# Second layer of an attention-plus-two-layers kernel: five nearly equal token groups, staging lent slot by slot, an operand store moved to GpSimd, weight sums a step ahead

## The chip, the core and the metric

The kernel runs on one NeuronCore of a Trainium2 chip. Five engines run side by side, each through its own queue in order: TensorE (PE in the profile; its weight loads are PEld), VectorE (DVE), ScalarE (ACT), GpSimd (POOL) and SyncE (SP), which here issues transfers only. A transfer (DMA) is issued by one of the queues and moved by 16 DMA engines. The metric is the device time of one execution in microseconds.

## The reference

Attention with a softmax over the feature axis of q and over the sequence axis of k, then two feed-forward layers on 4608 tokens of 512 features:

```python
kv = einsum('bhsd,bhse->bhde', softmax_seq(k), v)    # 8 x 8 heads, 576 x 64
x = einsum('bhsd,bhde->bhse', softmax_feat(q), kv)   # then heads side by side: 4608 x 512
x = square(relu(x @ w_in)) @ w_out       # first layer,  512 -> 2048 -> 512
h = x @ w_in2                            # second layer, 512 -> 2048
out = (h * sigmoid(h)) @ w_out2          #               2048 -> 512
```

All is float32. Each product on TensorE is made of three: both operands are split into a high part (rounded to the engine's float32r format) and the rest (low), and high x high, high x low and low x high are summed.

## The kernel before

The first layer runs in nine blocks of 512 tokens (`NB = 9`, `layer_in`, `layer_out`). It is not touched, except for what lies beside its last block.

The second layer multiplies 2 x 2 block matrices with seven products instead of eight (the Strassen-Winograd scheme): each operand has four quarters, and sums of quarters make up seven left operands (`PRODUCTS`: A11, S3, S2, S1, A12, A22, S4) and seven right ones (B11, T3, T2, T1, B21, N4, B22). Phase 2 is the product with `w_in2`, phase 3 the one with `w_out2`. Tokens are handled in groups `u`; the width of a group is the number of columns that stream through TensorE in one matmul. `supers` makes pairs of first-layer blocks, so that there are four groups of 512 columns and one of 256 (the ninth block alone). Each group has 56 steps in phase 2 and 56 in phase 3 (seven products x `NG = 8` feature groups `j`), and each step is six matmuls. So there are 2 x 56 x 6 = 672 matmuls for each group, 3360 in all: 2688 of 512 columns and 672 of 256. `LAST_LONG` puts the 256-column group fourth in phase 2 and a 512-column one last; in phase 3 the 256-column group is last.

Phase 2 goes by pairs of feature groups (`k` = 0, 1) and 14 steps for each pair (`PAIR`). `hidden_after` takes the results out of PSUM: products 0 and 2 are copied to four rooms that are kept for it (`keep`), product 1 to slot A22 of a tile `st` of seven slots; Silu follows, then the sums S1 to S4. A tile is stored to `g2d` by GpSimd in three transfers (2, 3 and 2 slots). `stpool` has two such tiles, one for each `k`: the next pair takes its tile at product 1 (`st[k] = stpool.tile(...)`), which waits until the stores of the pair before have landed. A function appended to `soon` runs one step later.

SBUF rooms of 512 columns (`NU = 89`) are lent and taken back in order. `a_load` fetches a left operand (SP), `a_split` makes its high part on ScalarE (tile `ah`) and its low part on VectorE (`al`, in place). Weights: `quarters` loads four quarters of a rounded weight from `wd` (SP), `weight_sums` makes T1, T2, T3 and N4 on GpSimd in one temporary (`wt`), and `weight_split` makes high and low parts (ScalarE, VectorE). `seven` does all that for one `j` of phase 2 beside the last block of the first layer. For phase 3 `raw_weights` loads and makes the first sums, and `product_weights` goes product by product through all `j` and makes the later sums between the splits. These are generators: each step of the loop advances those in `doing`, and starts others from `todo` while there is room. From the last block on (`pinned`) every engine's queue is in the order of the program.

Of the kernel before, what the change touches and what calls it, by code (L numbers as in the profile page):

```python
# [25 lines left out]
def kernel(  # L26
# [56 lines left out]
    P = 128  # L83
# [47 lines left out]
    def back(*ts):  # L131
# [7 lines left out]

    supers = [tuple(range(i, min(i + 2, NB))) for i in range(0, NB, 2)]  # L140
    NS = len(supers)
    x2d = [
        [dpool.tile([P, 7, len(bl) * HB], F32, name=f"x2d{u}_{e}") for e in range(2)]
        for u, bl in enumerate(supers)
    ]
    g2d = [
        [dpool.tile([P, 7, len(bl) * HB], F32, name=f"g2d{u}_{j}") for j in range(NG)]
        for u, bl in enumerate(supers)
    ]
# [114 lines left out]

    def weight_sums(w, t, which):

        b11, b21, b22 = (f32(w[n])[:, hi_] for n in (0, 4, 6))
        b12, s = t[:, lo_], t[:, hi_]
        if which == 0:
            gp.tensor_tensor(s, b12, b11, op=ALU.subtract)  # L270
            gp.tensor_tensor(b12, b22, b12, op=ALU.subtract)
        elif which == 1:
            gp.tensor_tensor(s, b22, s, op=ALU.subtract)
        else:
            gp.tensor_tensor(s, b21, s, op=ALU.subtract)

    def weight_split(ph, x, n, w, t):

        if n in w:
            src = f32(w[n])[:, hi_]  # L280
        else:
            w[n] = room(F32R, f"w{PRODUCTS[n][1]}")
            src = t[:, lo_ if n == 1 else hi_]
        ac.copy(w[n][:, lo_], src)
        ve.tensor_tensor(w[n][:, hi_], src, f32(w[n])[:, lo_], op=ALU.subtract)
        W[ph, x, n] = w[n]

    def seven(ph, x):

        w, t = quarters(ph, x)  # L290
        owed[0] += 4
        for _ in range(4):
            yield
        weight_sums(w, t, 0)
        yield
        for n in (0, 3, 1, 2, 4, 6, 5):
            if n in (3, 1, 2, 5):
                owed[0] -= 1
# [12 lines left out]

    def product_weights(ph, n):
        extra = n in (3, 2, 1, 5)
        owed[0] += NG * extra
        for x in range(NG):
            while x not in raws:
                yield
            w, t = raws[x]
            owed[0] -= extra
            weight_split(ph, x, n, w, t)  # L320
            if n in (3, 2):
                weight_sums(w, t, 1 if n == 3 else 2)
            if n == 5:
                back(t)
            yield
# [357 lines left out]
    def layer_out(i, f, n):  # L683
# [24 lines left out]
        sums(lambda s: t[:, :, s], ve)  # L708
        u, b = divmod(i, 2)
        for e in range(2):  # L710
            sp.dma_start(out=x2d[u][e][:, :, b * HB:(b + 1) * HB], in_=t[:, e])

# [14 lines left out]
    for i in range(NB - 1):  # L727
# [10 lines left out]

    LAST_LONG = [u for u in range(NS) if u != NS - 2] + [NS - 2]
    PAIR = (  # L740
# [10 lines left out]
    steps = [  # L751
        (2, u, n, 2 * p + k, u == LAST_LONG[-1])
        for u in LAST_LONG for p in range(NG // 2) for n, k in PAIR
    ]
    steps += [(3, u, n, j, u == NS - 1) for u in range(NS) for n, j in SUMMED]
    xs = {}

    def width(u):
        return len(supers[u]) * HB

    def a_load(ph, u, n, c):

        lo = room(F32R, "al")
        slot = PRODUCTS[n][0]
        w = width(u)
        src = (x2d if ph == 2 else g2d)[u][c]
        sp.dma_start(out=f32(lo)[:, 0:w], in_=src[:, slot])
        xs[ph, u, n, c] = [None, lo]
# [12 lines left out]
    soon = []  # L781

    def mm3(p, first, last, w, ws, hi, lo, cont):
        wh, wl = w[:, ws], w[:, HB + ws.start:HB + ws.stop]
        for m, (a, b) in enumerate(((wh, hi), (wh, lo), (wl, hi))):
            pe.matmul(
                p, a, b, start=first and m == 0, stop=last and m == 2, skip_group_check=cont
            )

    def step(ph, u, n, j, done):  # L790
        name, begins = INTO[n]
        w = width(u)
        now = soon[:]
        soon.clear()
        if ph == 2:
# [30 lines left out]
        if done:  # L826
            back(W.pop((ph, j, n)))

    def hidden_after(u, n, k, j):

        w = width(u)
        p = ps[INTO[n][0], k][:, 0:w]
        p0, u2 = (t[:, 0:w] for t in keep[k])
        to = g2d[u][j]
        if n == 1:
            st[k] = stpool.tile([P, 7, TB], F32, tag="st", name="st")
        t = st.get(k)
        at_ = lambda s: t[:, s, 0:w]

        def store(a, b):  # L840
            gp.dma_start(out=to[:, a:b], in_=t[:, a:b, 0:w])

        if n == 0:
            ac.copy(p0, p)
        elif n == 2:
            ac.copy(u2, p)
        elif n == 4:
            ve.tensor_tensor(p0, p, p0, op=ALU.add)
            back(ps.pop(("a", k)))
        elif n == 1:  # L850
            ac.copy(at_(A22), p)
            d = ps["d", k][:, 0:w]

            def then():
                ve.tensor_tensor(at_(A22), d, at_(A22), op=ALU.add)
                soon.append(lambda: ac.activation(at_(A22), at_(A22), AF.Silu))
            soon.append(then)
        elif n == 5:
            ac.activation(at_(A21), p, AF.Silu)
            back(ps.pop(("x", k)))  # L860
            ac.activation(at_(A11), p0, AF.Silu)
            store(A11, A22 + 1)

            def then():
                ve.tensor_tensor(at_(S1), at_(A21), at_(A22), op=ALU.add)
                ve.tensor_tensor(at_(S3), at_(A11), at_(A21), op=ALU.subtract)
                ve.tensor_tensor(at_(S2), at_(S1), at_(A11), op=ALU.subtract)
                store(S2, S3 + 1)
            soon.append(then)
        elif n == 6:  # L870
            ve.tensor_tensor(u2, p, u2, op=ALU.add)
            back(ps.pop(("d", k)))

            def then():
                ac.activation(at_(A12), u2, AF.Silu)

                def last():
                    ve.tensor_tensor(at_(S4), at_(A12), at_(S2), op=ALU.subtract)
                    store(A12, S4 + 1)
                soon.append(last)  # L880
            soon.append(then)

    def out_after(u, n, e, done):

        w = width(u)
        p = ps[INTO[n][0], e][:, 0:w]
        if n == 0:
            st[e] = stpool.tile([P, 7, TB], F32, tag="st", name="st")
        p0, u2, u3 = (st[e][:, s, 0:w] for s in (4, 5, 6))
# [8 lines left out]
        elif n == 1:  # L898
# [6 lines left out]
            soon.append(then)  # L905
        elif n == 6:
# [20 lines left out]
    def store(u, half, ends):  # L927
        w = width(u)
        t = st[half][:, 0:4].rearrange("p n c -> p (n c)")[:, 0:4 * w]
        o = out[supers[u][0] * TB:(supers[u][-1] + 1) * TB, :].rearrange(  # L930
            "(m j s r) (a f) -> a s r j m f", j=Q, s=2, r=2, f=P
# [101 lines left out]
    for what, n in order:  # L1033
        i, f = items[n]
        ends = i == NB - 1
        if what == "in":
            pinned[0] = ends
            if n == (NB - 1) * NF:
                assert nw == len(w2list) and not doing
                back(*kv_rooms[1:])  # L1040
                todo = [(8, lambda g=g: seven(2, g)) for g in range(NG)]
                todo[4:4] = [(4, lambda m=m: factor(LAST_LONG[0], m)) for m in FIRST_USE]
            if n == NF:
# [43 lines left out]

    keep.update({k: [room(F32, "keep") for _ in range(2)] for k in range(2)})
    for n, (ph, u, x, j, done) in enumerate(steps):
        if n == 0 or steps[n - 1][:2] != (ph, u):  # L1090
            if done and ph == 2:
                todo += [(4, lambda g=g: raw_weights(3, g)) for g in range(NG)]
# [4 lines left out]
            if ph == 3 and u == 0:  # L1097
                back(*keep[0], *keep[1])
        if ph == 2 and not done and (x, j) == (0, NG - 2):
            un = LAST_LONG[LAST_LONG.index(u) + 1]  # L1100
            todo += [(4, lambda m=m, un=un: factor(un, m)) for m in FIRST_USE]
        if ph == 2:
# [6 lines left out]
        spare = 0 if ph == 2 and not done else 2 if ph == 2 else max(2, AHEAD + SPLIT + 2 - 2 * len(xs))  # L1109
        while todo and len(doing) < 4 and len(rooms) - owed[0] >= todo[0][0] + spare:  # L1110
            begin()
    for fn in soon:
        fn()
    assert not todo and not doing
# [31 lines left out]
```

## Time and profile before

| | us |
|---|---|
| median of 3 runs (lowest, highest) | 1620.09 (1617.8, 1622.88) |
| the profiled execution | 1620.23 |
| its span, from the first to the last instruction | 1618.5 |
| TensorE busy in the span | 1565.8 (97%) |
| VectorE, ScalarE, GpSimd busy | 1050.2, 777.8, 182.4 |
| mean granted TensorE clock | 0.993 of full speed |

Times below are of the profiled execution, counted from its first instruction. What lies outside the span is 1620.23 - 1618.5 = 1.7 us. The second layer begins at 888.6 us. In a row of the timeline or the waits, what stands in brackets behind a row or after an arrow is the idle time of the engine before it, and what ended it.

### The profile page before, as it was taken

To read this page: it belongs to the slowest core of one execution; us is meant where nothing else is said; L and a number is where in the kernel's file an instruction comes from. 1 tells how busy PE (TensorE), PEld (TensorE's weight loads), DVE (VectorE), ACT (ScalarE), POOL (GpSimd) and SP (SyncE) were. 2 spreads that over 40 slices of the span, in tenths; PEclk is the share of its full clock that TensorE was granted. 3 is DMA by queue.
4 is the path that set the end of the run, shared out by engine and by line. 5 is a ranking of instruction groups with operands and counts; after the bars stand their busy time and mean duration, and the time that the engine had idled before them with its cause. 6 is when DMAs were issued, how large, how long until landed. Compare 5 with 4: busy or idle time off the path is not lost. (4 is left out here: it accounts for less than half of the span.)

```text
span 1618.5 us, 23420 instructions
## 1 busy us (share of the span) xinstructions
PE 1565.8 (97%) x7672; PEld 1290.4 (80%) x7672; DVE 1050.2 (65%) x2224; ACT 777.8 (48%) x1662; POOL 182.4 (11%) x397
## 2 busy tenths in 40 slices
PE   5999999999999999999999899999899899999998
PEld 3778888888878888888888788888887688888888
DVE  8999676676757767682354556565466955646555
ACT  6975343333434434342365445455455644544534
POOL 1000100100100010000031211111335100000000
PEclk9999999999999999999999999999999899999999
DMA  9634344352533434230051465756578659595856
GB/s 264 196 113 145 116 128 131 98 163 92 158 89 110 142 115 150 84 128 14 0 168 47 169 258 215 278 219 244 205 257 300 241 150 289 145 295 150 288 132 172
DMA packets 222458, 269.48 MB, mean 167 GB/s; under 512 B 60288, under 2 KB 158336, under 8 KB 222336
## 3 DMA queue, kind: packets, MB, share of 16 engines
q1 hardware_dynamic: 201264, 192.48, 39.3%
q0 software_dynamic: 18560, 74.46, 12.1%
q10 hardware_dynamic: 2512, 1.05, 0.3%
q8 instruction: 60, 0.98, 0.2%
q14 instruction: 62, 0.51, 0.1%
HBM read 160.17 MB, written 107.74 MB: 166 GB/s over the span
## 5 line engine op out<-in xcount | busy, mean ns | idle before, releaser
L73 PE MATMUL h<-x,wh 128*128 128x512 f32 x1152 | 359.6, 392 | 5.1 <-ACT wh L73 3.2
L73 PE MATMUL acc<-st,wh 128*128 128x512 f32 x1152 | 361.3, 393 | 0.2 <-DVE st L73 0.2
L73 DVE TENSOR_TENSOR al<-al,ah 128x512 fp32r<-128x512 f32 (+1 forms) x350 | 206.3, 636 | 137.4 <-ACT ah L73 134.9
L73 PEld LDWEIGHTS h<-x,wh 128*128 128x128 f32 x1152 | 215.4, 188 | 55.3 <-ACT wh L73 6.5
L73 PEld LDWEIGHTS acc<-st,wh 128*128 128x128 f32 x1152 | 213.2, 188 | 45.6 <-DVE st L73 1.6
L73 ACT CAST ah<-al 128x512 fp32r<-128x512 f32 (+1 forms) x350 | 188.3, 578 | 98.7 <-PE x L73 30.3
L73 PE MATMUL h<-x,wl 128*128 128x512 f32 x576 | 225.2, 391 | 0.2 <-DVE wl L73 0.2
L73 PE MATMUL acc<-st,wl 128*128 128x512 f32 x576 | 224.4, 390 | 0.0
L73 PE MATMUL x<-ah,wT 128*128 128x512 f32 (+1 forms) x640 | 191.3, 372 | 5.8 <-ACT keep L73 5.8
L73 ACT ACTIVATE g<-h 128x512 f32<-128x512 f32 x144 | 85.5, 594 | 175.8 <-PE h L73 175.2
L73 DVE TENSOR_TENSOR st<-g,st 128x512 fp32r<-128x512 f32 x144 | 99.9, 694 | 74.1 <-ACT st L73 66.5
L73 PEld LDWEIGHTS x<-ah,wT 128*128 128x128 f32 x640 | 117.8, 190 | 27.8 <-ACT keep L73 7.5
L73 DVE TENSOR_TENSOR st<-st 128x512 f32<-128x512 f32 (+1 forms) x196 | 122.8, 662 | 22.2 <-ACT st L73 16.3
L73 DVE TENSOR_TENSOR g<-g 128x512 f32<-128x512 f32 x112 | 76.8, 686 | 89.2 <-ACT g L73 88.9
L73 PEld LDWEIGHTS h<-x,wl 128*128 128x128 f32 x576 | 108.3, 188 | 24.1 <-DVE wl L73 1.7
L73 PEld LDWEIGHTS acc<-st,wl 128*128 128x128 f32 x576 | 108.2, 188 | 23.2
L73 ACT CAST st<-g 128x512 fp32r<-128x512 f32 x144 | 89.5, 621 | 74.0 <-DVE g L73 72.3
L73 PE MATMUL x<-al,wT 128*128 128x512 f32 (+1 forms) x320 | 118.7, 371 | 0.0
L73 PE MATMUL x<-ah,wN 128*128 128x512 f32 (+1 forms) x320 | 96.8, 374 | 6.9 <-ACT st L73 6.9
L73 PE MATMUL d<-ah,wB 128*128 128x512 f32 (+1 forms) x320 | 97.1, 376 | 4.9 <-DVE st L73 4.9
L73 ACT COPY st<-x 128x512 f32<-128x512 f32 (+1 forms) x70 | 38.0, 544 | 128.4 <-PE x L73 103.3
L73 POOL DMA_DIRECT2D g2d<-st x120 | 69.1, 578 | 263.4 <-ACT st L73 180.0
(128 smaller groups left out, 2439.9 us busy)
## 6 DMA issues: line engine op xcount, KB each, us to landing
al<-g2d SPq DMA_DIRECT2D x224, 256.0 KB, 3.9
g2d<-st POOLq DMA_DIRECT2D x64, 512.0 KB, 4.4
g2d<-st POOLq DMA_DIRECT2D x32, 768.0 KB, 5.0
wraw<-in_moe_w_in_dram SPq DMA_DIRECT2D x64, 256.0 KB, 3.0
wraw<-in_moe_w_out_dram SPq DMA_DIRECT2D x64, 256.0 KB, 3.2
x2d<-st SPq DMA_DIRECT2D x18, 896.0 KB, 6.0
al<-x2d SPq DMA_DIRECT2D x56, 256.0 KB, 4.6
v<-in_v_dram SPq DMA_DIRECT2D x64, 128.0 KB, 2.7
```

Source lines behind the costliest of these rows:

```text
L73: got = fn(*a, **kw)
```

## The change

1. The token axis is cut into five groups of 448, 448, 448, 448 and 512 columns (`sizes`, in units of 64 columns). The first layer's results lie in one DRAM tensor for each half (`x2d[e]`), and a group reads its columns from there. Phase 2 ends with the 512-column group, phase 3 takes the groups in the order 0, 1, 4, 2, 3.
2. The 14 slots of the two `st` tiles and one more room are lent singly (`slots`): each result takes the slot that has been free for longest, each sum is stored in a transfer of its own, and its slot goes back to the list. The four `keep` rooms are gone. For each `(u, j)` there are seven transfers to `g2d` in place of three (280 in place of 120 in all).
3. The store of the last block's results to `x2d` is issued by GpSimd, the others by SP as before.
4. The sums of weights are made earlier: in `seven` the first two at once, and the others two turns before they are split; in `raw_weights` all four, with a second temporary (`t2`), so that `product_weights` makes none.
5. Limits change: up to seven generators at a time in phase 2 before its last group, otherwise two (four before); `raw_weights` starts with 5 free rooms (4 before). Silu of A22 and of A12 is issued one and two steps later.

```diff
-    supers = [tuple(range(i, min(i + 2, NB))) for i in range(0, NB, 2)]
-    NS = len(supers)
+    GROUPS = NB * HB // (2 * Q)
+    NS = -(-NB // 2)
+    sizes = [GROUPS // NS + (u >= NS - GROUPS % NS) for u in range(NS)]
+    starts = [sum(sizes[:u]) * 2 * Q for u in range(NS + 1)]
+    x2d = [dpool.tile([P, 7, NB * HB], F32, name=f"x2d{e}") for e in range(2)]
...
-    def weight_sums(w, t, which):
+    def weight_sums(w, t, which, t2=None):
         b11, b21, b22 = (f32(w[n])[:, hi_] for n in (0, 4, 6))
         b12, s = t[:, lo_], t[:, hi_]
+        s2, s3 = (s, s) if t2 is None else (t2[:, lo_], t2[:, hi_])
+        a, b, to = ((b12, b11, s), (b22, b12, b12), (b22, s, s2), (b21, s2, s3))[which]
+        gp.tensor_tensor(to, a, b, op=ALU.subtract)
...
         weight_sums(w, t, 0)
-        yield
-        for n in (0, 3, 1, 2, 4, 6, 5):
+        weight_sums(w, t, 1)
+        for n in (None, None, 0, 3, 1, None, None, 2, 6, None, None, 5, 4):
...
     def raw_weights(ph, x):
         w, t = quarters(ph, x)
+        t2 = room(F32, "wt")
         for _ in range(6):
             yield
-        weight_sums(w, t, 0)
-        raws[x] = w, t
+        for m in range(4):
+            weight_sums(w, t, m, t2)
+            yield
+        yield
+        raws[x] = w, t, t2
...
-            weight_split(ph, x, n, w, t)
-            if n in (3, 2):
-                weight_sums(w, t, 1 if n == 3 else 2)
+            weight_split(ph, x, n, w, t2 if n in (2, 5) else t, (1, 2))
...
         for e in range(2):
-            sp.dma_start(out=x2d[u][e][:, :, b * HB:(b + 1) * HB], in_=t[:, e])
+            (gp if i == NB - 1 else sp).dma_start(
+                out=x2d[e][:, :, i * HB:(i + 1) * HB], in_=t[:, e]
+            )
...
+        def new(*names):
+            for x in names:
+                h[x] = slots.popleft()
+
+        def store(*which):
+            for s, x in which:
+                gp.dma_start(out=g2d[u][j][:, s], in_=h[x][:, 0:w])
+                slots.append(h.pop(x))
...
         elif n == 1:
-            ac.copy(at_(A22), p)
+            new("c22")
+            ac.copy(at_("c22"), p)
...
         elif n == 5:
-            ac.activation(at_(A21), p, AF.Silu)
+            new("c21", "s1", "s2")
+            ac.activation(at_("c21"), p, AF.Silu)
             back(ps.pop(("x", k)))
-            ac.activation(at_(A11), p0, AF.Silu)
-            store(A11, A22 + 1)
+            ac.activation(at_("c11"), at_("c11"), AF.Silu)
             def then():
-                ve.tensor_tensor(at_(S1), at_(A21), at_(A22), op=ALU.add)
+                ve.tensor_tensor(at_("s1"), at_("c21"), at_("c22"), op=ALU.add)
...
-                store(S2, S3 + 1)
+                store((A22, "c22"), (S1, "s1"), (S3, "c21"), (A11, "c11"))
...
+    slots.extend(st[e][:, s] for e in range(2) for s in range(7))
+    extra = room(F32, "extra")
+    slots.append(extra)
```

What moves on the queues, at the places that the prediction speaks of. Names end in buffer numbers; `wB11_8307`, `wt_8310` and their like are quarters of weights of one `j`, `st_157` before and `st_149` after is the tile with the last block's sums.

On SP, beside the last block of the first layer, before:

```order
L73 DMA wB21_8244<-wd2_5_129 128x256 [waits DMAHW5_49]
L73 DMA x2d4_0_82<-st_157 128x1792 [waits DMAHW6_49,DVE_49,Activation_49]
L73 DMA x2d4_1_83<-st_157 128x1792 [waits DMAHW7_49]
L73 DMA wB11_8307<-wd2_6_130 128x256 [waits DMAHW0_49,PE_49]
L73 DMA wt_8310<-wd2_14_138 128x256 [waits DMAHW1_49,PE_49]
```

On GpSimd, at the same place, after:

```order
L73 TENSOR_TENSOR wt_8234<-wB22_8233,wt_8234 128x256 [waits DMAHW4_49,Pool_49]
L73 TENSOR_TENSOR wt_8164<-wB21_8162,wt_8164 128x256 [waits DMAHW1_49,DVE_49]
L73 DMA x2d0_74<-st_149 896x1x256 [waits DVE_49,Activation_49]
L73 DMA x2d1_75<-st_149 896x1x256
L73 TENSOR_TENSOR wt_8234<-wB22_8233,wt_8234 128x256 [waits DVE_49]
L73 TENSOR_TENSOR wt_8234<-wB21_8232,wt_8234 128x256 [waits DMAHW5_49,DVE_49]
```

The loads of the seventh and eighth feature group's weights (`j` = 6, 7) no longer stand behind a store that waits for VectorE's sums; two sums of the sixth group's weights now stand behind it, on another queue.

On GpSimd, between the last two pairs of phase 2, sums of weights for phase 3, before:

```order
L73 DMA g2d3_5_113<-st_11086 128x1536 [waits DMASW7_49,DVE_49]
L73 TENSOR_TENSOR wt_10721<-wB22_10720,wt_10721 128x256 [waits DVE_49]
L73 TENSOR_TENSOR wt_10761<-wB22_10760,wt_10761 128x256 [waits DVE_49]
L73 DMA g2d3_4_112<-st_11075 128x1024 [waits DMASW0_49,DVE_49]
L73 TENSOR_TENSOR wt_10815<-wB22_10814,wt_10815 128x256 [waits DVE_49]
```

The same place after:

```order
L73 TENSOR_TENSOR wt_11174<-wB21_11167,wt_11174 128x256 [waits DMAHW1_49,Pool_49]
L73 DMA g2d4_5_113<-st_8300 128x512 [waits DMASW1_49]
L73 DMA g2d4_5_113<-st_8300 128x512 [waits DMASW2_49,Activation_49]
L73 DMA g2d4_5_113<-st_8301 128x512 [waits DMASW3_49,DVE_49]
L73 TENSOR_TENSOR wt_11237<-wt_11237,wB11_11234 128x256 [waits DMAHW3_49,DMAHW2_49,PE_49]
L73 TENSOR_TENSOR wt_11237<-wB22_11236,wt_11237 128x256 [waits DMAHW4_49,Pool_49]
L73 TENSOR_TENSOR wt_11242<-wB22_11236,wt_11237 128x256 [waits PE_49]
L73 TENSOR_TENSOR wt_11242<-wB21_11235,wt_11242 128x256 [waits DMAHW5_49,Pool_49]
```

Before, each sum waits for VectorE (a split that still reads the temporary), and sixteen of them stand behind the first splits; after, the sums wait for loads and for rooms that TensorE frees, and the last four of the 32 stand ahead of the last pair's stores.

## Rows read from the trace of the kernel before

**Rows 1.** The page, its head

```profile
span 1618.5 us, 23420 instructions
```

**Rows 2.** The chain: start, length, engine, tile, count of merged instructions

```profile
1289.79 10.88 PE x L73 x48
...
1592.83 5.76 PE x L73 x48
```

**Rows 3.** Windows by stage; PEclk is the granted clock

```profile
888.60:910.00 21.40, 16.78 (x62) 13.26 (x61) 10.81 (x20) 8.51 (x20) 3.88 (x5) 0.84 0.40 136
910.00:1125.30 215.30, 215.30 (x950) 177.80 (x949) 126.57 (x201) 109.38 (x204) 39.87 (x73) 1.00 0.61 233
1125.30:1176.40 51.10, 43.78 (x338) 42.38 (x337) 27.32 (x67) 23.52 (x68) 14.86 (x22) 0.97 0.68 241
1176.40:1250.00 73.60, 72.78 (x320) 59.61 (x319) 47.63 (x81) 40.97 (x89) 35.73 (x51) 1.00 0.79 279
1250.00:1280.00 30.00, 21.61 (x72) 15.12 (x71) 25.48 (x56) 18.99 (x48) 7.11 (x12) 0.83 0.52 180
1280.00:1572.50 292.50, 292.50 (x1292) 242.19 (x1291) 174.11 (x280) 139.18 (x245) 0.00 (x0) 1.00 0.71 214
1613.10:1618.50 5.40, 0.00 (x0) 0.00 (x0) 0.40 (x2) 0.00 (x0) 0.00 (x0) 0.73 0.45 97
```

**Rows 4.** TensorE's waits from 888 us on: total, times, longest

```profile
PE x L73 <- ACT st L73: 6.9, 6, 3.1
PE x L73 <- ACT keep L73: 5.8, 3, 4.6
PE d L73 <- DVE st L73: 4.9, 2, 4.4
PE x L73 <- DVE al L73: 2.9, 3, 2.1
```

**Rows 5.** Timeline, first pair: SP, then ScalarE (start, length)

```profile
870.16 0.97 SPq L73 DMA_DIRECT2D wB<-wd  x2
892.43 0.80 SPq L73 DMA_DIRECT2D x2d<-st  x2
...
899.67 0.40 ACT L73 CAST wB<-wB 128x256 fp32r<-128x256 f32 x1 [5.37 <-DMA wB<-wd]
```

**Rows 6.** Timeline, around the 256-column group: GpSimd, ScalarE, GpSimd

```profile
1129.79 1.05 POOL L73 DMA_DIRECT2D g2d<-st  x2 [2.83 <-ACT ah L73]
...
1134.08 0.37 ACT L73 COPY st<-x 128x256 f32<-128x256 f32 x1 [2.95 <-DMA g2d<-st]
...
1138.44 2.23 POOL L73 DMA_DIRECT2D g2d<-st  x3 [0.28 <-DVE st L73]
```

**Rows 7.** Timeline, from phase 2 to 3: VectorE, ScalarE, VectorE

```profile
1252.43 0.43 DVE L73 TENSOR_TENSOR wB<-wB 128x256 fp32r<-128x256 f32 x1 [0.83 <-POOL wt L73]
...
1255.68 0.63 ACT L73 ACTIVATE st<-st 128x512 f32<-128x512 f32 x1 [4.33 <-DVE st L73]
...
1278.10 0.68 DVE L73 TENSOR_TENSOR al<-al,ah 128x512 fp32r<-128x512 f32 x1
1278.70 0.42 DVE L73 TENSOR_TENSOR wN<-wt,wN 128x256 fp32r<-128x256 f32 x1
1279.03 0.68 DVE L73 TENSOR_TENSOR al<-al,ah 128x512 fp32r<-128x512 f32 x1
```

**Rows 8.** Groups by form: busy us, mean ns, idle before

```profile
L73 DVE TENSOR_TENSOR wT<-wt,wT 128x256 fp32r<-128x256 f32 x48 | 24.4, 526 | 1.0 <-ACT wT L73 0.9
...
L73 DVE TENSOR_TENSOR wN<-wt,wN 128x256 fp32r<-128x256 f32 x16 | 6.6, 417 | 1.6 <-ACT wN L73 1.6
...
L73 POOL TENSOR_TENSOR wt<-wB,wt 128x256 f32<-128x256 f32 x48 | 39.9, 838 | 50.9 <-DVE wT L73 49.6
```

**Rows 9.** DMA issues: KB each, median us to landing

```profile
g2d<-st POOLq DMA_DIRECT2D x64, 512.0 KB, 4.4
g2d<-st POOLq DMA_DIRECT2D x32, 768.0 KB, 5.0
...
x2d<-st SPq DMA_DIRECT2D x18, 896.0 KB, 6.0
...
g2d<-st POOLq DMA_DIRECT2D x16, 256.0 KB, 3.4
```

More of the change, by code (lines that the diff above doesn't have):

```diff
@@ L137 @@
     qd = [dpool.tile([P, TB], F32, name=f"qd{c}") for c in range(KC)]
-    supers = [tuple(range(i, min(i + 2, NB))) for i in range(0, NB, 2)]
-    NS = len(supers)
[L142 to L145, printed above, removed]
+    GROUPS = NB * HB // (2 * Q)
[3 more added lines that the diff above has]
+    x2d = [dpool.tile([P, 7, NB * HB], F32, name=f"x2d{e}") for e in range(2)]
     g2d = [
-        [dpool.tile([P, 7, len(bl) * HB], F32, name=f"g2d{u}_{j}") for j in range(NG)]
-        for u, bl in enumerate(supers)
+        [dpool.tile([P, 7, n * 2 * Q], F32, name=f"g2d{u}_{j}") for j in range(NG)]
+        for u, n in enumerate(sizes)
     ]
@@ L294, in seven @@
         weight_sums(w, t, 0)
-        yield
-        for n in (0, 3, 1, 2, 4, 6, 5):
-            if n in (3, 1, 2, 5):
-                owed[0] -= 1
-            weight_split(ph, x, n, w, t)
+        weight_sums(w, t, 1)
+        for n in (None, None, 0, 3, 1, None, None, 2, 6, None, None, 5, 4):
+            if n is not None:
+                if n in (3, 1, 2, 5):
+                    owed[0] -= 1
+                weight_split(ph, x, n, w, t)
             if n in (3, 2):
-                weight_sums(w, t, 1 if n == 3 else 2)
+                weight_sums(w, t, 2 if n == 3 else 3)
             yield
@@ L317, in product_weights @@
                 yield
-            w, t = raws[x]
+            w, t, t2 = raws[x]
             owed[0] -= extra
-            weight_split(ph, x, n, w, t)
-            if n in (3, 2):
-                weight_sums(w, t, 1 if n == 3 else 2)
+            weight_split(ph, x, n, w, t2 if n in (2, 5) else t, (1, 2))
+            if n == 1:
+                back(t)
             if n == 5:
-                back(t)
+                back(t2)
             yield
@@ L736 @@
                     at(i, s + d, fn, nxt, pr)
-    LAST_LONG = [u for u in range(NS) if u != NS - 2] + [NS - 2]
+    ORDER3 = [u for u in range(NS) if sizes[u] == sizes[-1]]
+    ORDER3 = [u for u in range(NS) if u not in ORDER3][:2] + ORDER3 + [u for u in range(NS) if u not in ORDER3][2:]
     PAIR = (
@@ L751 @@
     steps = [
-        (2, u, n, 2 * p + k, u == LAST_LONG[-1])
-        for u in LAST_LONG for p in range(NG // 2) for n, k in PAIR
+        (2, u, n, 2 * p + k, u == NS - 1)
+        for u in range(NS) for p in range(NG // 2) for n, k in PAIR
     ]
-    steps += [(3, u, n, j, u == NS - 1) for u in range(NS) for n, j in SUMMED]
+    steps += [(3, u, n, j, u == ORDER3[-1]) for u in ORDER3 for n, j in SUMMED]
     xs = {}
     def width(u):
-        return len(supers[u]) * HB
+        return sizes[u] * 2 * Q
     def a_load(ph, u, n, c):
@@ L765, in a_load @@
         w = width(u)
-        src = (x2d if ph == 2 else g2d)[u][c]
-        sp.dma_start(out=f32(lo)[:, 0:w], in_=src[:, slot])
+        src = x2d[c][:, slot, starts[u]:starts[u + 1]] if ph == 2 else g2d[u][c][:, slot]
+        sp.dma_start(out=f32(lo)[:, 0:w], in_=src)
         xs[ph, u, n, c] = [None, lo]
@@ L781, with later, due @@
     soon = []
+    def later(fn, n=1):
+        soon.append([n, fn])
+    def due():
+        for x in soon:
+            x[0] -= 1
+        now = [x[1] for x in soon if x[0] <= 0]
+        soon[:] = [x for x in soon if x[0] > 0]
+        return now
     def mm3(p, first, last, w, ws, hi, lo, cont):
@@ L792, in step @@
         w = width(u)
-        now = soon[:]
-        soon.clear()
+        now = due()
         if ph == 2:
@@ L827, in step @@
             back(W.pop((ph, j, n)))
+    slots = deque()
     def hidden_after(u, n, k, j):
@@ L832, in hidden_after @@
         p = ps[INTO[n][0], k][:, 0:w]
[L833 to L841, printed above, removed]
+        h = keep.setdefault(k, {})
+        def new(*names):
[5 more added lines that the diff above has]
+                slots.append(h.pop(x))
@@ L843, in hidden_after @@
+        at_ = lambda x: h[x][:, 0:w]
         if n == 0:
-            ac.copy(p0, p)
+            new("c11")
+            ac.copy(at_("c11"), p)
         elif n == 2:
-            ac.copy(u2, p)
+            new("c12")
+            ac.copy(at_("c12"), p)
         elif n == 4:
-            ve.tensor_tensor(p0, p, p0, op=ALU.add)
+            ve.tensor_tensor(at_("c11"), p, at_("c11"), op=ALU.add)
             back(ps.pop(("a", k)))
         elif n == 1:
-            ac.copy(at_(A22), p)
+            new("c22")
+            ac.copy(at_("c22"), p)
@@ L852, in hidden_after @@
             d = ps["d", k][:, 0:w]
             def then():
[L855 to L857 removed]
+                ve.tensor_tensor(at_("c22"), d, at_("c22"), op=ALU.add)
+                later(lambda: ac.activation(at_("c22"), at_("c22"), AF.Silu), 2)
+            later(then)
         elif n == 5:
[L859 removed]
+            new("c21", "s1", "s2")
@@ L872, in hidden_after @@
             back(ps.pop(("d", k)))
+            mine = keep.pop(k)
             def then():
-                ac.activation(at_(A12), u2, AF.Silu)
+                a12, s2 = (mine[x][:, 0:w] for x in ("c12", "s2"))
+                ac.activation(a12, a12, AF.Silu)
                 def last():
[L878 to L881, printed above, removed]
+                    s4 = slots.popleft()
+                    ve.tensor_tensor(s4[:, 0:w], a12, s2, op=ALU.subtract)
+                    for s, t in ((S2, mine["s2"]), (A12, mine["c12"]), (S4, s4)):
+                        gp.dma_start(out=g2d[u][j][:, s], in_=t[:, 0:w])
+                        slots.append(t)
+                later(last)
@@ L883, in out_after @@
+            later(then, 3)
     def out_after(u, n, e, done):
@@ L904, in then @@
                 turn(u, 0, 2 + e, u3)
-            soon.append(then)
+            later(then)
         elif n == 6:
@@ L929, in store @@
         t = st[half][:, 0:4].rearrange("p n c -> p (n c)")[:, 0:4 * w]
-        o = out[supers[u][0] * TB:(supers[u][-1] + 1) * TB, :].rearrange(
+        o = out[2 * starts[u]:2 * starts[u + 1], :].rearrange(
             "(m j s r) (a f) -> a s r j m f", j=Q, s=2, r=2, f=P
@@ L1041 @@
                 todo = [(8, lambda g=g: seven(2, g)) for g in range(NG)]
-                todo[4:4] = [(4, lambda m=m: factor(LAST_LONG[0], m)) for m in FIRST_USE]
+                todo[4:4] = [(4, lambda m=m: factor(0, m)) for m in FIRST_USE]
             if n == NF:
@@ L1086, in stream @@
                 fn(*steps[m][:4])
-    keep.update({k: [room(F32, "keep") for _ in range(2)] for k in range(2)})
+    st.update({e: stpool.tile([P, 7, TB], F32, tag="st", name="st") for e in range(2)})
+    slots.extend(st[e][:, s] for e in range(2) for s in range(7))
+    extra = room(F32, "extra")
+    slots.append(extra)
     for n, (ph, u, x, j, done) in enumerate(steps):
@@ L1091 @@
             if done and ph == 2:
-                todo += [(4, lambda g=g: raw_weights(3, g)) for g in range(NG)]
+                todo += [(5, lambda g=g: raw_weights(3, g)) for g in range(NG)]
                 todo += [
@@ L1096 @@
                 ]
-            if ph == 3 and u == 0:
-                back(*keep[0], *keep[1])
+            if ph == 3 and u == ORDER3[0]:
+                back(extra)
         if ph == 2 and not done and (x, j) == (0, NG - 2):
-            un = LAST_LONG[LAST_LONG.index(u) + 1]
-            todo += [(4, lambda m=m, un=un: factor(un, m)) for m in FIRST_USE]
+            todo += [(4, lambda m=m, u=u: factor(u + 1, m)) for m in FIRST_USE]
         if ph == 2:
@@ L1109 @@
         spare = 0 if ph == 2 and not done else 2 if ph == 2 else max(2, AHEAD + SPLIT + 2 - 2 * len(xs))
-        while todo and len(doing) < 4 and len(rooms) - owed[0] >= todo[0][0] + spare:
+        while todo and len(doing) < (7 if ph == 2 and not done else 2) and len(rooms) - owed[0] >= todo[0][0] + spare:
             begin()
-    for fn in soon:
-        fn()
+    assert not soon
     assert not todo and not doing
```

22 lines of the change are left out of this document (6 added, 16 removed).

## Prediction

> **What bounds the kernel now.** I read the page's head first, then the windows by stage, the chain, TensorE's waits, and the timelines at the three places where it waits. The page gives a span of 1618.5 us [rows 1]. TensorE's work in the second layer is paced by its stream of matmuls: where the chain runs along TensorE alone, 48 matmuls of 512 columns take 10.88 us, 226.7 ns each, and 48 of 256 columns take 5.76 us, 120.0 ns each [rows 2]. With 2688 of the one and 672 of the other the second layer needs 609.3 + 80.6 = 689.9 us. It takes 724.5, from 888.6 to the border of the last window at 1613.1 [rows 3]. So 34.6 us are lost, and the windows show where. From 910.0 to 1125.3 and from 1280.0 to 1572.5 TensorE is busy throughout, at full clock: nothing is to be had there. The loss lies in four windows (each counts a matmul that straddles its border, so my parts fall short of the whole by some 2 us):
> - 888.6 to 910.0, the first pair of phase 2: 21.4 - 62 x 0.2267 = 7.3 us;
> - 1125.3 to 1176.4, the 256-column group in phase 2: 51.1 - 338 x 0.120 = 10.5 us;
> - 1176.4 to 1250.0: 73.6 - 320 x 0.2267 = 1.1 us;
> - 1250.0 to 1280.0, where phase 2 turns into phase 3: 30.0 - 72 x 0.2267 = 13.7 us.
>
> TensorE waits there for ScalarE's copies out of PSUM (`st`, `keep`) and for VectorE (`st`, `al`), 20.5 us in 14 waits [rows 4]. The clock adds to it: it was granted at 0.84, 0.97 and 0.83 of full speed in three of these windows [rows 3], some 10 us in all (0.16 x 21.4 + 0.03 x 51.1 + 0.17 x 30.0), and it falls to its lower level, 1.2 GHz, only around the longest of these waits. Where a wait goes, its clock loss goes too.
>
> **The change, part by part.** *Widths.* The two rows give (226.7 - 120.0) / 256 = 0.417 ns for a column and 13.3 ns for a matmul. By that line 448 columns take 200.0 ns. Then 2688 x 200.0 + 672 x 226.7 = 537.6 + 152.3 = 689.9 us: as many matmuls, as many columns, the same sum. A weight load at every matmul would be the risk, but the 256-column groups run at 120 ns with the same loads, so 200 is no floor. The cut into equal groups is worth only what it does to waits. The same holds for splits and copies: their number stays, and so does their sum of columns.
>
> *The 256-column group.* Its loss comes from the staging tile. ScalarE's copy waits 2.95 us for a store to `g2d` [rows 6], in every pair. The tile is taken again at product 1, 7 steps after the step that issues the last store of the pair before. At 256 columns that is 7 x 6 x 0.120 = 5.0 us, and a store's landing (3.4 to 5.0 us [rows 9]) with its way through the queue uses it up; at 512 it is 9.5 us, and no wait shows. A step of 448 columns takes 6 x 0.200 = 1.20 us. With single slots in order of age I count, from the program, at least 6 steps between a slot's store and its next use (7.2 us), 7 (8.4 us) where a copy that TensorE needs takes it. GpSimd issues 14 transfers for a pair where it issued 6. One with one row per partition takes 0.53 us (two in 1.05), one of two or three slots 0.74 (three in 2.23) [rows 6]; 14 x 0.53 = 7.4 us in a pair of 16.8. A burst is eight stores, 4.2 us. The 224 KB transfer is nearest to the row of 256 KB, 3.4 us; behind half a burst it lands about 5.5 us after it could be issued, inside 7.2. I take the whole 10.5 us as gained, and nothing lost elsewhere; bounds: 10.5 gained, or 2.6 us lost in each of 20 pairs (the fourth rival).
>
> The Trainium skill (DMA: Bandwidth & Descriptors, "Anatomy of one DMA — SWDGE (gpsimd) path") gives each such transfer about 2.0 us of fixed cost and the rest by bytes, 2.5 us for 224 KB by estimate; that speaks against seven stores in place of three. The rows lie higher (3.4 for 256 KB, 5.0 for 768 KB), but show the same: most of it is fixed. By the rule as by the rows it matters only if the stores wait for each other.
>
> *The first pair.* SP issues two loads at 870.2, then nothing until 892.4: it holds at the last block's `x2d` store, which waits for VectorE's sums. The weights behind it come late, and ScalarE, in order, stands 5.37 us at a split of one of them at 899.67 with TensorE's copies behind it [rows 5]. After, these loads wait for rooms only, and arrive long before. GpSimd holds at the store instead, until 892.4, and the sum behind it feeds one split on ScalarE. The two issues are 896 rows each; by the growth from 128 to 384 rows [rows 6] 1.2 us each, bounds 0.53 and 1.6. So the sum ends at about 892.4 + 2.4 + 0.75 = 895.6 (GpSimd's sums take 0.84 in the mean, 0.75 undisturbed), the split at 895.9, and TensorE's next copy at 896.9. TensorE needs it at step 7: 888.6 + 7 x 1.20 = 897.0. Just in time. Gain 7.3, bounds 3 and 7.7.
>
> *From phase 2 to 3.* VectorE waits 0.83 us again and again for a GpSimd sum, because sum and split take turns at one temporary; ScalarE then stands 4.33 us for VectorE [rows 7], and TensorE behind it. All 32 sums are now made before the last pair's stores. VectorE's remaining work, from the tail of the third pair to the split of phase 3's step 28, is in its queue 16 tiles of 512 columns (0.64 us each, between the 0.60 of the row and a dependent one), 56 weight splits (0.33) and 29 `al` of 448 (0.53, between 0.33 for 256 and 0.60 for 512 [rows 7]): 10.2 + 18.5 + 15.4 = 44 us. TensorE takes 12 x 1.36 + 28 x 1.20 = 49.9 for it. ScalarE has less per step. So they keep up, with splits made 6 steps (7.2 us) ahead. A split that runs beside a sum takes 526 ns, one without 417 [rows 8]; the sums move to where VectorE has time. I take 13.7 + 1.1 as gained but give back 2.5 us for small waits there and in the first pair, which this count can't see (bounds 0 and 9: a step short of splits in every third of the 28).
>
> *The end.* The last group is 448 columns wide, not 256. Two transposes grow by 0.2 us, and the last stores by 393 KB: at the 97 GB/s of the last window [rows 3] 4.0 us, at the 214 of phase 3 1.8. That window's rate is low because issue and landing fill it; I take 1.8 with the transposes (bounds 0.2 and 4.2).
>
> *Sum* against the profiled execution, 1620.2 us: - 34.6 + 2.5 + 1.8 = 1589.9. It stands 0.1 above the median, so 1590 for the median too.
>
> **Rivals.**
> - *Phase 3 still starts short of splits.* VectorE is the busiest engine there (25.5 of 30 us [rows 3]), and TensorE's steps get shorter. For it: the waits for `al` [rows 4]. Against: those came after a long stall. Half of 13.7 stays: 1597.
> - *GpSimd takes over the wait of the first pair*, since my margin is 0.1 us and the store's landing (6.0 us [rows 9]) frees the second tile's slots at about 901, when they are wanted. 4 us stay: 1594.
> - *Only the group's waits go*; the other two come back in another place: 1620.2 - 10.5 + 1.8 = 1611.
> - *Slower: stores too slow for the slots.* If a store takes over 7.2 us from issue to landing, VectorE's in-order queue holds in each of 20 pairs. It decides at 34.6 / 20 = 1.7 us in a pair, so at about 9 us to landing. The 5.0 us of 768 KB speaks against it, the burst of eight, on a queue that also makes sums, for it. With 2.6 us in a pair, as the 256-column group lost: 1590 + 52 = 1642. That is also what the page's rule would bring if the fixed costs came one behind the other.
> - *Nothing moves*, because the waits of one kind give way to others of equal size: 1620.
>
> **How the numbers follow.** The forecast (1586 to 1595) 0.62; phase 3 short of splits 0.16; GpSimd in the first pair 0.10; only the group's waits 0.05; slower 0.04; nothing 0.03. The prediction is the forecast's 1590. The range takes in the first three, with low 1586 (no small waits, the shortest tail) and high 1601 (the phase-3 rival with the long tail); it leaves out 0.12 above and a little below. Within 0.3% is 4.9 us, about what a measurement of this kernel can tell from no change: faster 0.93 (the first four), same 0.03, slower 0.04.
>
> **What would show it.** Right: windows of 448 columns with TensorE busy throughout and 48 matmuls in 9.6 us; no wait of TensorE over 1 us from 888 on; a granted clock of 1.00 from there to the end; SP's loads of weights without a gap between 870 and 892; no wait of VectorE for GpSimd's sums in phase 3; a last window of 7 us. Wrong: ScalarE waiting for stores in the middle of the 448-column groups (the fourth rival), `al` before phase 3's first 16 steps (the first), ScalarE for GpSimd near 895 (the second), or matmuls of 448 columns far from 200 ns apart, which would take the ground from the sum.

## The result, and the profile after

The changed kernel takes 1598.42 us in the median of four runs (1596.48 to 1599.27); the kernel before took 1618.94 beside it. The ratio is 0.9869, with a 95% interval of 0.9847 to 0.9891: faster by 1.3%. The forecast was 1590, with 1586 to 1601 as the range. The profiled execution took 1597.86 us, its span is 1596.1.

The windows of the changed kernel by stage, in the columns of [rows 3] (length, then busy us and instructions of TensorE's matmuls, its weight loads, VectorE, ScalarE, GpSimd; granted clock, DMA share, GB/s):

```profile
888.50:910.00 21.50, 21.50 (x107) 19.91 (x107) 17.40 (x31) 13.41 (x33) 13.21 (x18) 1.00 0.51 174
910.00:1160.00 250.00, 249.83 (x1233) 231.17 (x1233) 149.58 (x262) 128.76 (x263) 109.47 (x206) 1.00 0.67 241
1160.00:1237.60 77.60, 77.60 (x345) 64.37 (x344) 48.60 (x77) 39.07 (x77) 54.92 (x88) 1.00 0.84 296
1237.60:1262.00 24.40, 23.53 (x114) 20.58 (x113) 24.36 (x57) 23.76 (x65) 6.96 (x13) 1.00 0.76 257
1262.00:1588.10 326.10, 326.01 (x1569) 294.23 (x1567) 195.78 (x346) 152.80 (x291) 0.00 (x0) 1.00 0.68 208
1588.10:1596.10 8.00, 0.00 (x0) 0.00 (x0) 0.60 (x1) 0.00 (x0) 0.00 (x0) 0.71 0.57 115
```

TensorE is busy nearly throughout (in the fourth window 0.87 of 24.40 us are idle), and the clock is at its full level in every window up to the last matmul. Its waits from 880 us on, the answer to [rows 4], are three short lines, 1.0 us in all where the four lines there add up to 20.5:

```profile
PE d L73 <- DVE al L73: 0.6, 2, 0.3
PE x L73 <- DVE al L73: 0.2, 1, 0.2
PE x L73 <- ACT st L73: 0.2, 1, 0.2
```

So the four losses are gone, but for the small waits counted below. What is short of the forecast stands in the chain (start, length, engine, tile, matmuls merged), the answer to [rows 2]:

```profile
1258.91 9.73 PE x L73 x48
...
1297.82 19.46 PE x L73 x96
...
1386.54 10.88 PE d L73 x48
```

The first two rows are of 448 columns: 202.7 ns for each matmul, not 200.0. The third is of 512, 226.7 as before. The excess is no wait: in the steady stretches five spacings follow each other without end, 199, 207, 202, 203 and 202 ns. With these the layer's matmuls need 2688 x 0.2027 + 672 x 0.2267 = 697.1 us. It takes 699.5 (888.5 to 1588.0), so 2.4 us are small waits, and 8.0 us follow the last matmul where 5.4 did [rows 3].

The first pair, by the timelines of SyncE, GpSimd and ScalarE, the answer to [rows 5]:

```profile
870.07 10.60 SPq L73 DMA_DIRECT2D wB<-wd  x3
883.30 0.32 SPq L73 DMA_DIRECT2D wt<-wd  x1
...
892.85 2.01 POOL L73 DMA_DIRECT2D x2d<-st  x2 [5.91 <-DVE wT L73]
894.56 1.07 POOL L73 TENSOR_TENSOR wt<-wB,wt 128x256 f32<-128x256 f32 x1
...
895.66 0.41 ACT L73 CAST wT<-wt 128x256 fp32r<-128x256 f32 x1 [3.95 <-POOL wt L73]
895.98 0.40 ACT L73 CAST wB<-wB 128x256 fp32r<-128x256 f32 x1
896.28 0.96 ACT L73 COPY st<-x 128x448 f32<-128x448 f32 x2
```

SyncE goes on issuing weights between 870 and 892, in bursts, as rooms come free. GpSimd now stands at the store, and ScalarE stands 3.95 us for the sum behind it. Its copies start at 896.28, and TensorE does not wait.

### The profile page after: what moved, and what is told of

The parts are those of the page before. It is cut to its first block, busy times and chain, and to the rows that moved or that the text cites. A ratio compares the mean times of both kernels' runs of the same rounds, so it can differ in the third digit from the quotient of the medians.

```text
span 1596.1 us, 23648 instructions
## 1 busy us (share of the span) xinstructions
PE 1564.0 (98%) x7672; PEld 1331.7 (83%) x7672; DVE 1046.4 (66%) x2224; ACT 774.2 (49%) x1662; POOL 265.0 (17%) x559
## 4 chain that ended last, share of the span: by engine, by line
PE 67%; DVE 3%; issue 1%; DMA 1%; SPq 1%; POOL 0%; ACT 0%; DVEq 0%; ACTq 0%; POOLq 0%
PE x L73 23%; PE acc L73 13%; PE h L73 12%; PE d L73 12%; PE a L73 6%; DVE st L73 1%; PE xps L73 1%; SPq L73 1%; PE kvps L73 0%; DVE wT L73 0%; DMA al<-g2d 0%; DVE al L73 0%; DVE wu L73 0%; DVE wB L73 0%; DMA wraw<-in_moe_w_out_dram 0%
## 5 line engine op out<-in xcount | busy, mean ns | idle before, releaser
L73 DVE TENSOR_TENSOR al<-al,ah 128x448 fp32r<-128x448 f32 (+1 forms) x350 | 205.4, 635 | 120.9 <-ACT ah L73 118.5
L73 ACT CAST ah<-al 128x448 fp32r<-128x448 f32 (+1 forms) x350 | 188.0, 579 | 93.2 <-PE x L73 26.1
L73 PE MATMUL x<-ah,wT 128*128 128x448 f32 (+1 forms) x640 | 193.2, 370 | 0.2 <-ACT st L73 0.2
L73 ACT COPY st<-x 128x448 f32<-128x448 f32 (+1 forms) x142 | 76.8, 544 | 199.3 <-PE x L73 182.3
L73 POOL DMA_DIRECT2D g2d<-st x261 | 139.7, 541 | 140.8 <-ACT st L73 77.7
L73 DVE TENSOR_TENSOR st<-st 128x448 f32<-128x448 f32 (+1 forms) x169 | 108.7, 671 | 28.4 <-ACT st L73 23.9
L73 PE MATMUL x<-al,wT 128*128 128x448 f32 (+1 forms) x320 | 118.4, 370 | 0.0
L73 PE MATMUL a<-ah,wB 128*128 128x448 f32 (+1 forms) x320 | 100.5, 370 | 0.0
L73 PE MATMUL d<-ah,wT 128*128 128x448 f32 (+1 forms) x320 | 96.5, 370 | 0.0
```

Source lines behind the costliest of these rows:

```text
L73: got = fn(*a, **kw)
```

## Experiments

Two things were to be settled. One is why 448 columns are off the line: (theory 1) the width itself, (theory 2) disturbance by transfers and other engines, (theory 3) the place of the operands. The other is which edit took which loss away. Each timed kernel is compared with the kernel before on its own chip:

| run | median us | ratio to before, 95% interval |
|---|---|---|
| changed kernel | 1598.42 | 0.9869 [0.9847, 0.9891] |
| e2_cut_384 | 1588.17 | 0.9810 [0.9797, 0.9824] |
| e3_old_cut | 1587.37 | 0.9806 [0.9793, 0.9820] |
| e4_store_sp | 1606.04 | 0.9909 [0.9895, 0.9923] |
| e5_late_sums | 1612.74 | 0.9960 [0.9946, 0.9974] |
| e6_old_cut_old_staging | 1602.22 | 0.9890 [0.9877, 0.9903] |
| e7_equal_old_staging | 1606.02 | 0.9919 [0.9899, 0.9940] |

**Widths alone (e1_widths).** A stream of matmuls and nothing else:

```
for width in (512, 496, 480, 464, 456, 448, 440, 432, 416, 400, 384, 352, 320, 288, 256, 192, 128):
    stream(f"w{width}", width, 96)
stream("off64", 448, 96, off=64)
stream("poff64", 448, 96, poff=64)
stream("still", 448, 96, still=True)
p = stream("last", 448, 96)
```

> No part of the layers is computed: six matmuls a step in the order of the second layer (high by high, high by low, low by high, for two halves), from operands that stay in SBUF, with nothing running beside them, 96 matmuls at each of 17 widths from 512 to 128 columns. Theory 1, the width itself is slow on TensorE: the 448-column stream is 202 to 203 ns apart with the same five spacings in turn as in the changed kernel (199, 207, 202, 203, 202), while 512 and 256 stay at 226.7 and 120.0; which other widths leave the straight line is then read from this run. Theory 2, the transfers and the other engines disturb it in the kernel: 448 columns are 200.0 ns apart here. Theory 3, the place of the operands or of the sum does it: the two 448-column streams that start 64 columns further in (in SBUF, in PSUM) differ from the plain one.

Measured, as the mean distance of the starts in the trace from the third matmul of each width on, beside the line of [rows 2] (0.417 ns for a column and 13.3). Each width is entered from the next wider one:

| columns | 512 | 496 | 480 | 464 | 456 | 448 | 440 | 432 | 416 | 400 | 384 | 352 | 320 | 288 | 256 | 192 | 128 |
|---|---|---|---|---|---|---|---|---|---|---|---|---|---|---|---|---|---|
| ns | 226.7 | 220.0 | 216.6 | 210.0 | 208.7 | 206.7 | 200.0 | 195.7 | 188.3 | 180.0 | 173.7 | 161.1 | 146.6 | 131.7 | 120.0 | 111.6 | 111.7 |
| line | 226.7 | 220.0 | 213.3 | 206.7 | 203.3 | 200.0 | 196.7 | 193.3 | 186.7 | 180.0 | 173.3 | 160.0 | 146.7 | 133.3 | 120.0 | 93.3 | 66.7 |

The chain has the four last streams, all of 448 columns: 64 columns further in in SBUF, in PSUM, with the same weights loaded again each time, and plain:

```profile
342.43 19.89 PE off L84 x96
362.32 19.84 PE poff L84 x96
382.16 19.84 PE still L84 x96
402.00 19.85 PE last L84 x96
```

So the width itself is slow, with nothing running beside it: theory 2 fell, and so did theory 3 for the two shifts tried. 512, 496, 400, 384, 320 and 256 are on the line, the widths between 496 and 400 above it, 352 a little above and 288 a little below it, and below 256 it holds no more. But this run gave 206.7 for 448, not the kernel's 202.7, which theory 1 had not foreseen; the last two experiments are about that.

**Other cuts (e2_cut_384, e3_old_cut).** Only the widths of the groups and their order in phase 3 differ from the changed kernel:

```
-    sizes = [GROUPS // NS + (u >= NS - GROUPS % NS) for u in range(NS)]
-    ORDER3 = [u for u in range(NS) if sizes[u] == sizes[-1]]
-    ORDER3 = [u for u in range(NS) if u not in ORDER3][:2] + ORDER3 + [u for u in range(NS) if u not in ORDER3][2:]
+    sizes = [8, 8, 6, 6, 8]
+    ORDER3 = [0, 1, 4, 2, 3]
```

and in e3 these two lines in their place (a unit is 64 columns):

```
+    sizes = [8, 8, 8, 4, 8]
+    ORDER3 = [0, 1, 2, 4, 3]
```

> The changed kernel with groups of 512, 512, 384, 384 and 512 columns, phase 3 in the order 0, 1, 4, 2, 3, so that no matmul has 448 columns and a group of 384 is last. Theory 1 (448 columns are slow by themselves): 2688 matmuls lose their 3.5 ns, 9.4 us, and the end after the last matmul is a little shorter: 1588 us, if 384 is on the line (173.3 ns). Theory 2 (disturbance): the excess stays, 1597 to 1599. Rival to both: at 384 columns a step has 14% less time for the same splits and copies, and waits come back: 1592 to 1600 with waits of TensorE in the two groups of 384.

> The changed kernel with the old widths (512, 512, 512, 256, 512, the 256 last in phase 3); lent slots, the store on GpSimd and the early weight sums stay. If the equal groups are what removed the 10.5 us of waits in the group of 256: those waits are back, the excess at 448 columns (9.4 us) and 2.7 us of the end are gone: 1597 us. If the slots alone removed them: 1586 us, the best so far. If the group of 256 lengthens more than before, as its sums now want fifteen slots: above 1600.

(The 3.5 ns and 9.4 us of these expectations count the small waits in; the steady excess is 2.7 ns, 7.2 us.)

e2 gave 1588.17 where 1588 was expected. Its two groups of 384 columns in phase 2, by the windows:

```profile
1040.10:1156.60 116.50, 116.50 (x674) 116.50 (x673) 71.28 (x139) 61.40 (x138) 58.03 (x110) 1.00 0.70 248
```

674 matmuls in 116.5 us is 172.9 ns (173.3 by the starts) with no idle time, so the rival of waits at 384 fell too. e3 gave 1587.37; of the three cases that were set down, the one with 1586 came. Its group of 256, to be held against the third of [rows 3], and its end:

```profile
1120.70:1161.70 41.00, 40.80 (x337) 40.39 (x336) 27.48 (x67) 23.88 (x66) 27.61 (x52) 1.00 0.78 279
1583.90:1589.40 5.50, 0.00 (x0) 0.00 (x0) 0.48 (x2) 0.00 (x0) 0.00 (x0) 0.94 0.44 95
```

51.1 us have become 41.0 with the same widths: the group's waits go without the cut into equal groups; that it is the staging which takes them away, e6 shows below. Beside it the equal groups bring nothing, and cost 11 us (1598.42 - 1587.37): 7.6 in the second layer (699.5 against 691.9, from 892.0 to 1583.9), 2.5 at the end (8.0 against 5.5), and 0.9 that these two traces don't place. (The first layer ends anywhere from 887.0 us, in e7, to 892.2, in e4, and the difference is there by 500 us, long before the place that these edits change; so second layers are best compared by their own length.) Both versions beat the changed kernel; their intervals overlap each other.

**The staging of before (e6_old_cut_old_staging, e7_equal_old_staging).** `hidden_after` and its tiles as they were, once with the old widths, once with the equal groups:

```
-    slots.extend(st[e][:, s] for e in range(2) for s in range(7))
...
+    keep.update({k: [room(F32, "keep") for _ in range(2)] for k in range(2)})
...
-            new("c22")
-            ac.copy(at_("c22"), p)
+            ac.copy(at_(A22), p)
```

> The run with the old widths (1587 us), with the staging of before as well: a tile of seven slots for each j, four tiles kept for the sums, three stores. If lending slot by slot is what removed the waits in the group of 256, they are back: 10.5 us and about 1598 us. If the store on GpSimd or the earlier weight sums removed them: 1587 us.

> The changed kernel (448, 448, 448, 448, 512) with the staging of before. If equal groups are enough by themselves, since no group is short: 1598 us, as the changed kernel. If the staging needs the lent slots at 448 columns too: 1602 us or more, with waits of TensorE for banks or sums in every group.

e6 is back at 1602.22, 0.84% or 13.6 us above e3 by the ratios. Its group of 256 in phase 2, and the largest of TensorE's waits:

```profile
1121.50:1172.00 50.50, 44.02 (x337) 43.00 (x336) 27.87 (x69) 24.33 (x70) 15.38 (x22) 0.94 0.69 246
```

```profile
PE x L73 <- ACT st L73: 5.8, 4, 2.9
```

That is 9.5 us more than in e3 for 337 matmuls, and the wait of [rows 4] by name. ScalarE's copies in this group wait for stores to `g2d` again, as in [rows 6]: four times, 7.8 us in all, up to 3.5; in e3 never. e6 puts the whole staging back, though: the lending by slots, the seven stores in place of three and the later Silu were not tried one by one. A part of the remaining 4 us lies at the change of phase (141 matmuls in 35.0 us where e3 makes 151). e7 came out at 1606.02, 0.5% or 8 us above the changed kernel: at 448 columns too the old staging makes TensorE wait, though for single pairs and not in every group as expected:

```profile
887.20:1164.00 276.80, 273.70 (x1346) 252.18 (x1346) 166.88 (x292) 143.55 (x295) 77.63 (x103) 1.00 0.65 233
...
1240.80:1270.00 29.20, 25.87 (x121) 21.73 (x120) 28.03 (x63) 22.82 (x62) 3.69 (x7) 1.00 0.66 225
```

At 202.7 ns these windows would take 272.8 and 24.5 us. So the equal groups are no substitute for the slots, and lose against the old widths with either staging.

**The store back on SyncE (e4_store_sp).**

```
-            (gp if i == NB - 1 else sp).dma_start(
+            sp.dma_start(
```

> The changed kernel with the last block's two operand stores back on SyncE's queue. If they were what made the first pair late, as the prediction had it: 7.3 us come back, 1606 us, with SyncE's loads of the first group behind the stores and TensorE waiting between 888 and 912. If the narrower first group had already taken that wait away, or GpSimd's queue holds it up as much: 1597 to 1600.

1606.04: 7.6 us above the changed kernel by the medians, 6.5 by the ratios; in the traces the second layer is 5.8 us longer (705.3 against 699.5), and the rest of their difference lies in the first layer. The timelines of SyncE and ScalarE, and TensorE's wait:

```profile
896.27 1.23 SPq L73 DMA_DIRECT2D x2d<-st  x2
897.60 1.38 SPq L73 DMA_DIRECT2D wB<-wd  x1
...
904.64 0.40 ACT L73 CAST wB<-wB 128x256 fp32r<-128x256 f32 x1 [3.53 <-DMA wB<-wd]
...
907.24 0.40 ACT L73 CAST wB<-wB 128x256 fp32r<-128x256 f32 x1 [2.20 <-DMA wB<-wd]
```

```profile
PE x L73 <- ACT st L73: 3.3, 1, 3.3
```

The weight's load leaves only behind the store, ScalarE stands for it twice, and TensorE stands 3.3 us; from 907.3 to 914.1, from the end of that wait on, the clock was granted at its lower level of 1.2 GHz, and fifteen matmuls start 373 ns apart in place of 203, which with the slow ones at either end costs about 3 us more. The prediction's chain of causes for this pair is seen in each link.

**The weight sums late again (e5_late_sums).**

```
-        for m in range(4):
-            weight_sums(w, t, m, t2)
-            yield
...
+        weight_sums(w, t, 0)
+        weight_sums(w, t, 1)
...
+            weight_split(ph, x, n, w, t)
+            if n in (3, 2):
+                weight_sums(w, t, 2 if n == 3 else 3)
```

> The changed kernel with phase 3's weight sums made as before, inside the splits of the product that needs them, in one tile of work space, and up to four jobs at a time in the last group of phase 2 and in phase 3. If the prediction's term is right, the 13.7 us at the change of phase are back: 1612 us, with waits of TensorE for wT and wN between 1240 and 1275. If the wait came from elsewhere (the splits themselves, or the slots of the last group): 1598 to 1602.

1612.74: 14.3 us above the changed kernel by the medians; in the traces the second layer is 12.6 us longer (712.0 against 699.5). The run also puts back the limits of four generators and four free rooms, so it prices the early sums together with these. VectorE's timeline, ScalarE's, and TensorE's wait:

```profile
1235.52 0.43 DVE L73 TENSOR_TENSOR wB<-wB 128x256 fp32r<-128x256 f32 x1 [0.83 <-POOL wt L73]
...
1240.65 0.42 DVE L73 TENSOR_TENSOR wB<-wB 128x256 fp32r<-128x256 f32 x1 [0.83 <-POOL wt L73]
...
1242.91 0.63 ACT L73 ACTIVATE extra<-extra 128x512 f32<-128x512 f32 x1 [7.89 <-DVE extra L73]
```

```profile
PE d L73 <- DVE extra L73: 8.8, 1, 8.8
```

VectorE waits 0.83 us for one sum after the other, as in [rows 7]; the sum of a product (`extra`) behind it in its queue is late, and TensorE stands 8.8 us for it in phase 2's last group, not for `wT` and `wN` as my expectation named them. The clock was at 1.2 GHz from 1238.8 to 1249.1, so the matmuls behind the wait start 427 ns apart, not 227.

**The beat at 448 columns (e8_448_beside, e9_448_entry).** e8 puts a condition of the kernel beside each stream; e9 changes only the width that ran before:

```
stream("plain", 448, 32)
stream("line", 512, 8)
stream("again", 448, 32)
stream("tiles", 448, 32, tiles=8)
stream("evict", 448, 32, tiles=8, evict=True)
...
stream("both", 448, 32, tiles=8, evict=True, beside=split)
```

```
for x, use in (("a", first), ("b", second), ("c", first)):
    for width in (512, 456, 128, 496, 440, 256):
        stream("entry", width, 8, use)
        p = stream(f"{x}from", 448, 16, use)
```

> No part of the layers is computed: 192 matmuls of 448 columns for each of nine conditions. The stream by itself was 206.7 ns apart in the run of the widths, and is 202.7 in the changed kernel. If the kernel's faster beat comes from operands in many tiles, the stream named tiles is at 202.7 and those behind it as well; if it comes from sums that are copied out, or from splits or loads beside it, only evict, split, load or both are; if it depends on what ran before, the stream that follows 512 columns (again) differs from the one that follows the warm-up (plain) or the last. If none differs from 206.7, the cause is none of these.

> No part of the layers is computed: 96 matmuls of 448 columns, entered each time from 48 matmuls of another width (512, 456, 128, 496, 440, 256 columns in turn), once with operands at the places of the first run of widths, once with another set, once more with the first. If the beat (206.7 or 202.7 ns) is caught from the stream before, 448 after 512 is at 202.7 and 448 after 456 or 128 at 206.7, with either set. If it hangs on where the operands lie, the first set gives 206.7 throughout and the second may give 202.7. If all are alike, neither is the cause.

The chain of e8, 192 matmuls in a row:

```profile
63.78 38.91 PE plain L90 x192
...
152.50 38.91 PE tiles L90 x192
...
308.15 38.91 PE both L90 x192
```

202.7 ns, and the same in the five streams of 448 between and behind them, so copies, splits, loads and the number of tiles do nothing to this beat. The chain of e9, its first round (512, 456, 128 and 496 columns ahead of 448):

```profile
54.26 10.88 PE entry L90 x48
65.14 19.45 PE afrom L90 x96
84.59 10.01 PE entry L90 x48
94.60 19.83 PE afrom L90 x96
114.43 5.31 PE entry L90 x48
119.74 19.89 PE afrom L90 x96
139.62 10.72 PE entry L90 x48
150.35 19.46 PE afrom L90 x96
```

After 512 or 496 columns (and after 440 and 256) 96 matmuls of 448 take 19.45 to 19.48 us, 202.7 ns each; after 456 or 128 they take 19.83 to 19.89, 206.7 each, to the end of the stream. The second and third rounds, the second with other operands, show the same. The beat is caught from the stream before and kept while nothing interrupts the stream. (In e5's kernel the first matmuls of phase 3 start 206.7 ns apart, and 202.7 behind a gap of 1.6 us.) In the kernel a 448-column group comes after 512 columns, hence 202.7.

## Why the prediction was right, and where it was off

- **Direction and mechanism: right.** Of the 34.6 us of waits and lost clock all but 2.4 are gone. e4 and e5 return two of the terms, the first pair (forecast 7.3, returned 5.8 to 7.6) and the change of phase (13.7, returned 12.6 to 14.3); e3 beside e6 returns the third, the group of 256 (10.5; 9.5 in its window).
- **The range: held by luck.** 1598.4 lies above the forecast's 1586 to 1595, the case that had 0.62. It lies under 1601 only because the range made room for phase 3 starting short of splits and for a long tail. The first came at a fifth of its price; what filled the room was the width, for which the sum had no bound at all.
- **The mis-sized term: the width.** "By that line 448 columns take 200.0 ns" failed: 202.7, so 2688 x 2.7 ns = 7.2 us that the sum didn't have. Two points make a line only if nothing bends between them, and e1 shows that 480 to 440 lie above it. The text weighed a weight load as the only risk, and named "far from 200 ns" as what would take the ground away: 1.3% was enough to move the time by 0.45%.
- **"The cut into equal groups is worth only what it does to waits":** it was worth less. The prediction gave the group's 10.5 us to the staging, which e3 and e6 confirm, and took the cut as free but for 1.8 us at the end; it costs 11 us.
- **Small waits:** 2.5 forecast, 2.4 measured. Half of them lie in 1237.6 to 1262.0, where VectorE is busy 24.36 of 24.40 us and ScalarE, which "has less per step" by the prediction, 23.76: the rival that phase 3 starts short of splits came, at a fifth of its price (24.4 - 114 x 0.2027 = 1.3 us, against half of 13.7).
- **First pair:** the sum's end was forecast for 895.6 and came at 895.63, the copy for 896.9 and came at 896.28, against a need at 897.0. The sign set down for the second rival was there (ScalarE stood 3.95 us for GpSimd's sum), its price was not, as TensorE did not wait. That SyncE would load "without a gap" was wrong: it waits for rooms, and nobody waits for it.
- **The end:** 1.8 forecast, 2.6 measured (8.0 against 5.4), within the bounds. SyncE's four last stores take 2.92 us to issue in the changed kernel and 1.77 in the kernel before; I had counted their bytes, not their issue.
- **The slower rival:** a store of 224 KB lands 3.6 us after its issue (median of 208), well short of the 7.2 us that a slot has. The estimate from the Trainium skill (DMA: Bandwidth & Descriptors, "Anatomy of one DMA — SWDGE (gpsimd) path") was 2.5; the measurement stands. With the 2.0 us of fixed cost that the Trainium skill gives there, one behind the other, 14 stores would take 28 us by estimate in a pair of 16.8, a loss far above the 2.6 us that the prediction set beside that rule; no run shows them so. ScalarE waits for a store's slot at times, the sign set down for this rival (five waits of up to 2.2 us between 910 and 1240), but TensorE's only wait for a copy is the 0.2 us shown above.

Together: 1589.9 + 7.2 - 0.1 + 0.8 = 1597.8, against 1597.86 in the profiled execution.

## What to carry to other kernels

A wait is best taken away where it arises: the new staging did it at every width tried (512 with 256, 512 with 384, 448), while evening out the group widths hid part of it and cost more than it hid. Before a tile's width is changed, measure the pace of a stream at that very width, entered as the kernel enters it; 2.7 ns on each of 2688 matmuls took back a fifth of the 34.6 us of waits. Of the versions tried, the old widths with the lent slots, the moved store and the early sums (e3) and the cut with 384 in place of 448 (e2) are 1.9% faster than the kernel before.

## What the runs showed of the hardware

- The distance of matmuls, each with its own weight load, is not linear in the columns: 480, 464, 456, 448 and 440 take 3.3 to 6.7 ns more (432 and 416 2.4 and 1.6) than the line through 512 and 256 when they follow each other in e1, while 496, 400, 384, 320 and 256 lie on it within 0.4 ns. The Trainium skill (TensorE: Matmul & The Clock Gate, "Wait — 56ns, not 53.3ns?") gives, for matmuls back to back, columns by the clock and some 2.5 ns for each matmul: by estimate 189.2 ns at 448 and 215.8 at 512. It says nothing there of a weight load at each matmul. The runs here differ, 202.7 and 226.7, and decide.
- Below 256 columns the distance no longer falls: 111.6 ns at 192 and 111.7 at 128.
- The same stream has two steady beats, 202.7 and 206.7 ns at 448 columns, and keeps the one in which the stream before left it as long as nothing interrupts it (e9; for an interruption, e5). 496 columns do the like: 220.0 ns behind 512 in e1, 223.3 behind 448 in e9 (10.72 us for 48). Why one width leaves it in the one and another in the other is open.
